# One group of four heads' keys and queries: transposed on TensorE, or loaded as token rows and transposed by DMA

## The chip, the cores and the metric

The kernel runs on one core of a Trainium2 chip. The metric is the device time of one execution in microseconds (us), as the median of several runs. A profile is one further execution with every instruction recorded.

## The reference

Causal attention with an additive bias that falls with a running sum, followed by a layer norm and a two-layer network with a residual. Batch 8, 8 heads, 576 tokens, 64 dimensions per head, model width 512, hidden width 2048.

```python
def _attn_ref(q, k, v, s):
    scores = scale * np.matmul(q, k.transpose(0, 1, 3, 2))
    cum = np.cumsum(np.maximum(s, 0.0), axis=-1)
    bias = -(cum[:, :, :, None] - cum[:, :, None, :])
    scores = np.where(causal, -1000000000.0, scores + np.minimum(bias, 0.0))
    scores = scores - np.max(scores, axis=-1, keepdims=True)
    attn = np.exp(scores)
    attn = attn / (np.sum(attn, axis=-1, keepdims=True) + 1e-09)
    return np.matmul(attn, v)
def _moe_ref(x, g_ln, w_ch1, w_ch2):
    xn = (x - mu) / np.sqrt(var + 1e-06) * g_ln
    return x + np.maximum(xn @ w_ch1, 0.0) @ w_ch2
```

For the scores TensorE needs q and k with the 64 dimensions of a head (and four rows that carry the bias) on the partitions and the tokens along the free axis. In memory they lie the other way round: tokens outside, dimensions inside. So every head's q and k have to be transposed somewhere.

## The kernel before

The order of the work is written out by hand: one loop over `n` (line 745), 64 steps, one for each head of each batch (`b, h = n // 8, n % 8`). A step emits `pre(n)` (line 675), which holds loads and casts for later steps; then the scores of its head (`scores`, line 304, three PSUM banks called `sa`, `sb`, `sc`, each turned into weights `er` by an exponential on ACT, line 323, and masked by POOL, line 331); then pieces of the network of the batch before (`run_units`: `mlp1` writes `ph`, line 497; `mlp2` writes `py`, line 515, and DVE finishes the rows in `yo`, line 524, which SP stores, line 542); and from step 10 on the product with the values of the head two steps back (`pv`, line 378, matmuls at line 389). Every engine and every DMA queue executes its instructions in the order in which they are written.

Heads go in groups of four, `gam = n // 4` (16 groups). A group's q and k stand transposed in one of two buffers, `kq[gam % 2]`, 68 partitions high: 64 dimensions and four rows of bias. There are two ways to fill it.

- **By TensorE** (groups 0 to 5, that is batches 0 to 2). Two heads at a time, "pairs" `g`, two pairs to a group. `ld_cast_pair` (line 130) has POOL issue two DMAs, k and q, which load f32 and write bf16, six consecutive tokens to a partition (96 partitions). `tr_pair` (line 243) issues 12 transposes on TensorE (line 255) into two PSUM tiles `trqk`; `evac_pair` (line 262) copies them to `kq` in four copies, for the later pairs two on DVE (line 100) and two on ACT (line 98). `PAIR_LOADS` (line 671) says in which step a pair is loaded, `PAIRS` (line 672) in which it is transposed. The bias rows come by four small DMAs on SP, `aug` (line 207; lines 210 and 212), which wait until the group before in the same buffer has been read.
- **By DMA** (groups 6 to 15). `ld_rows` (line 159) loads 128 tokens of four heads, k and q, with two DMAs on SP (line 164) into a staging tile `rowtmp`, from the pool of six that the values' loads (`vtmp`, line 139) use too. `cast_rows` (line 172) has POOL cast it to bf16 (line 176) and copy the bias columns next to it (line 177) into one of four `rows` buffers. `tr_rows` (line 182) issues one DMA transpose on SP (line 186), 128 tokens by 8 head-halves, into `kq`. A group needs five of each; steps `4 gam - 6` to `4 gam - 2` hold them (lines 706 to 721). The transposed tiles lie tile by tile, so a range of queries that runs past token 512 is read with two matmuls in place of one (`q_cols`, line 289).

`NPE = 3` (line 49) is the number of batches that go by TensorE. The four `rows` buffers get their unused columns zeroed once, by POOL, in step 16 (line 701). `cT`, the bias columns, is filled in steps 9 and 12.

Of the kernel before, what the change touches and what calls it, by code (L numbers as in the profile page):

```python
# [19 lines left out]
def kernel(  # L20
# [25 lines left out]
    EW = 1664  # L46
    G = 4
    NG = BH // G
    NPE = 3
    NM = 10  # L50
    NR = 4
    QT = 6
# [77 lines left out]
    def ld_cast_pair(g):  # L130
        ld_cast("k", g)
        ld_cast("q", g)

    def ld_v(b, t):
        if b >= B:
            return
        pn = P if t < NF else TL
        tmp = stage.tile([P, H, D], F32, name="vtmp", tag="st")
        nc.sync.dma_start(
            out=tmp[:pn], in_=v[b, :, t * P : t * P + pn, :].rearrange("h s d -> s h d")  # L140
        )
        loaded["v", b, t] = tmp


    def ld_cast_v(b, t):
        pn = P if t < NF else TL
        nc.gpsimd.dma_start(
            out=v_bf[b % 2][:pn, t, :, 0:D],
            in_=v[b, :, t * P : t * P + pn, :].rearrange("h s d -> s h d"),
        )  # L150

    def cast_v(b, t, eng):
        if b >= B:
            return
        pn = P if t < NF else TL
        copy_on(eng, v_bf[b % 2][:pn, t, :, 0:D], loaded.pop(("v", b, t))[:pn])


    def ld_rows(gam, t):
        pn = P if t < NF else TL  # L160
        b, h0 = gam // 2, (gam % 2) * G
        tmp = stage.tile([P, 2, G, D], F32, name="rowtmp", tag="st")
        for u, src in enumerate((k, q)):
            nc.sync.dma_start(
                out=tmp[0:pn, u],
                in_=src[b, h0 : h0 + G, t * P : t * P + pn, :].rearrange("h s d -> s h d"),
            )
        loaded["rows", gam, t] = tmp
# [3 lines left out]
    def cast_rows(gam, t):  # L172
        pn = P if t < NF else TL
        r = rows[turn[0] % NR]
        turn[0] += 1
        nc.gpsimd.tensor_copy(out=r[0:pn, :, :, 0:D], in_=loaded.pop(("rows", gam, t))[0:pn])  # L176
        nc.gpsimd.tensor_copy(
            out=r[0:pn, :, :, D:KA], in_=cT[0:pn, t, :, gam * G : (gam + 1) * G, :]
        )
        ready["rows", gam, t] = r  # L180

    def tr_rows(gam, t):
        pn = P if t < NF else TL
        r = ready.pop(("rows", gam, t))
        o = t * 2 * G * P
        nc.sync.dma_start_transpose(
            out=kq[gam % 2]
            .rearrange("p u h s -> p (u h s)")[:, o : o + 2 * G * pn]
            .rearrange("p (h s) -> p h s", s=pn),
            in_=r[0:pn].rearrange("p u h c -> p (u h c)"),  # L190
        )
# [4 lines left out]
    def ld_w1(c):  # L196
        sl = slice(c * 512, (c + 1) * 512)
        nc.gpsimd.dma_start(out=w1_bf[:, :, sl], in_=w1_r[:, :, sl])

    def ld_w2(i):  # L200
        nc.gpsimd.dma_start(
            out=w2_bf[:, 4 * i : 4 * i + 4, :], in_=w2_r[:, 4 * i : 4 * i + 4, :]
        )
# [3 lines left out]
    def aug(gam, eng, h0=0):  # L207
        r = slice(gam * G + h0, gam * G + G)
        i = gam % 2
        eng.dma_start(out=kq[i][D : D + 1, 1, h0:G, 0:S], in_=c_hi[r, :])  # L210
        for j in range(3):
            eng.dma_start(out=kq[i][D + 1 + j : D + 2 + j, 0, h0:G, 0:S], in_=c3[r, j, :])
# [62 lines left out]
    def qk_pair(g, k_engs, q_engs):  # L275
        tr_pair(g)
        evac_pair("k", g, k_engs)
        evac_pair("q", g, q_engs)


    def k_cols(b, h, kb):
        i, hh = (b * 2 + h // G) % 2, h % G
        if b < NPE:
            return kq[i][0:KA, 0, hh, kb * P : (kb + 1) * P]
        n = P if kb < NF else TL
        o = kb * 2 * G * P + hh * n
        return kq[i].rearrange("p u h s -> p (u h s)")[0:KA, o : o + P]

    def q_cols(b, h, q0, q1):
        i, hh = (b * 2 + h // G) % 2, h % G  # L290
        if b < NPE:
            return [(q0, q1, kq[i][0:KA, 1, hh, q0:q1])]
        flat = kq[i].rearrange("p u h s -> p (u h s)")
        full = flat[0:KA, 0 : NF * 2 * G * P].rearrange("p (t h s) -> p t h s", t=NF, s=P)
        o = NF * 2 * G * P + (G + hh) * TL
        got = []
        if q0 < NF * P:
            qf = min(q1, NF * P)
            got.append((q0, qf, full[:, q0 // P : qf // P, G + hh, :]))
        if q1 > NF * P:  # L300
            got.append((NF * P, q1, flat[0:KA, o : o + TL]))
        return got

    def scores(b, h):
        e = er[:, h % 4, :]
        pe_mask = b * H + h < NM

        def bank(name, blocks, o):
            a = ps_s.tile([P, 512], F32, name=name, tag="s")
            for c, kb, q0, q1, diag in blocks:  # L310
                for a0, a1, cols in q_cols(b, h, q0, q1):
                    nc.tensor.matmul(  # L312
                        a[:, c + a0 - q0 : c + a1 - q0],
                        lhsT=k_cols(b, h, kb),
                        rhs=cols,
                        start=True,
                        stop=not (pe_mask and diag),
                    )
                if pe_mask and diag:
                    nc.tensor.matmul(  # L320
                        a[:, c : c + P], lhsT=ident, rhs=maskT, start=False, stop=True
                    )
            nc.scalar.activation(out=e[:, o : o + 512], in_=a, func=ACT.Exp, scale=scale)  # L323

        bank("sa", ((0, 0, 0, 512, True),), 0)
        bank("sb", ((0, 0, 512, 576, False), (64, 1, 128, 576, True)), OB)
        bank("sc", ((0, 2, 256, 576, True), (320, 3, 384, 576, True)), OC)
        if pe_mask:
            return
        for o in (0, OB + 64, OC, OC + 320):  # L330
            nc.gpsimd.affine_select(  # L331
                out=e[:, o : o + P],
                in_=e[:, o : o + P],
                compare_op=ALU.is_ge,
                fill=0.0,
                base=0,
                pattern=[[1, P]],
                channel_multiplier=-1,
            )
# [328 lines left out]

    PAIR_LOADS = {11: 8, 12: 9, 13: 10, 16: 11}
    PAIRS = {9: 5, 11: 6, 13: 7, 14: 8, 15: 9, 16: 10, 21: 11}


    def pre(n):
        if n == 0:
            nc.vector.memset(mhalf, -0.5)
            ld_cast_pair(4)
        elif n == 1:
            ld_w1(1)  # L680
        elif n == 3:
            ld_cast_pair(5)
            for t in range(NT):
                ld_cast_v(1, t)
        elif n == 4:
            ld_w1(2)
            ld_w1(3)
        elif n == 7:
            ld_cast_pair(6)
            ld_w2(0)  # L690
            ld_cast_pair(7)
            ld_w2(1)
        elif n == 10:
            ld_w2(2)
            ld_w2(3)
        elif n == 12:
            nc.vector.memset(cT[:, :, 0, :, 0], -1.0)
            nc.vector.memset(cT[:, :, 1, :, 1:4], 1.0)
        elif n == 16:
            for r in rows:  # L700
                nc.gpsimd.memset(r[:, :, :, KA:P], 0.0)
        if n in PAIR_LOADS:
            ld_cast_pair(PAIR_LOADS[n])
        if n % 4 == 0 and 2 <= n // 4 + 1 < 2 * NPE:
            aug(n // 4 + 1, nc.sync)
        for gam in range(2 * NPE, NG):
            m = n - 4 * gam
            if m == -6:
                ld_rows(gam, 0), ld_rows(gam, 1)
            elif m == -5:  # L710
                cast_rows(gam, 0), cast_rows(gam, 1)
                ld_rows(gam, 2), ld_rows(gam, 3)
            elif m == -4:
                tr_rows(gam, 0), tr_rows(gam, 1)
                cast_rows(gam, 2), cast_rows(gam, 3)
                ld_rows(gam, 4)
            elif m == -3:
                tr_rows(gam, 2), tr_rows(gam, 3)
                cast_rows(gam, 4)
            elif m == -2:  # L720
                tr_rows(gam, 4)
        for nb in range(2, B):
            m = n - H * nb + (5 if nb == 2 else 7)
            if 0 <= m < NT:
                ld_v(nb, m)
            if 1 <= m <= NT:
                cast_v(nb, m - 1, "pool")
# [17 lines left out]
    for n in range(BH):  # L745
        b, h = n // H, n % H
# [62 lines left out]
        nu = (2 if n < 16 else -(-len(queue) // (end - n + 1))) - 2  # L809
        if n in PAIRS:  # L810
            qk_pair(PAIRS[n], ("dve", "dve"), ("act", "act"))
        scores(b, h)
# [63 lines left out]
```

## Time and profile before

| What | Value |
|---|---|
| median of 5 runs | 368.65 us (367.83 to 372.14) |
| the profiled execution's own time | 367.83 us |
| its span, first to last instruction | 366.1 us |
| PE busy | 357.7 us, 98% of the span |
| DVE, ACT, POOL busy | 205.8, 194.2, 161.5 us |
| granted TensorE clock | 1.0 |
| DMA packets | 147981, of which 134185 under 512 bytes |

PE is TensorE's matmuls, PEld its weight loads, DVE VectorE, ACT ScalarE, POOL GpSimd; SPq is the queue of DMAs that SyncE issues. Times in a timeline are microseconds from the start of the span. In a timeline's line stand the start, the duration of the merged pieces, the engine, the line of the kernel, the operation, the tile written and the tiles read, the shape and the count; a bracket at the end is the idle time of the engine before it, and what ended it. A matmul's recorded duration includes its way through the pipeline, so the pace of TensorE is read from the distance between starts.

### The profile page before, as it was taken

Reading aid. Unit: us, or ns where it says so; the run is one execution under the profiler, and the core shown is the slowest. Engines: PE = TensorE matmul, PEld = TensorE weight load, DVE = VectorE, ACT = ScalarE, POOL = GpSimd, SP = SyncE. Lnnn points to the kernel's source line nnn. Section 1 sums busy time; section 2 is a strip of 40 time slices with the busy share of each in tenths; the row PEclk is TensorE's granted clock in tenths of the full one; section 3 lists DMA queues with packets and bytes.
Section 4 is the critical chain, followed back from the end, with each engine's and each line's share of the span. In section 5 each row is a group of like instructions: output and inputs, shape, how many; then the busy total and the mean of one; then the engine's idle time right before and its main releaser. Section 6 shows DMA issues by size and latency. Waiting matters only on the chain.

```text
span 366.1 us, 8372 instructions
## 1 busy us (share of the span) xinstructions
PE 357.7 (98%) x3079; PEld 197.7 (54%) x3079; DVE 205.8 (56%) x539; ACT 194.2 (53%) x371; POOL 161.5 (44%) x441
## 2 busy tenths in 40 slices
PE   8999999999999999999999999999999999999995
PEld 3676555565555555555555555555555554444444
DVE  7697789786448453944394547643665483112211
ACT  5895998568733674357534753476347422501410
POOL 8954475757643646454754563555552101000000
PEclk9999999999999999999999999999999999999999
DMA  8999994679965999599869998898730011011013
GB/s 149 161 193 182 202 214 74 136 194 171 178 134 134 215 189 186 116 242 178 182 160 221 181 183 141 201 206 185 146 100 2 0 60 57 3 57 57 3 29 86
DMA packets 147981, 50.42 MB, mean 138 GB/s; under 512 B 134185, under 2 KB 143268, under 8 KB 147940
## 3 DMA queue, kind: packets, MB, share of 16 engines
q1 hardware_dynamic: 129364, 40.74, 52.3%
q0 software_dynamic: 18176, 8.62, 19.4%
q10 hardware_dynamic: 400, 0.52, 0.5%
q8 instruction: 24, 0.39, 0.4%
q14 instruction: 17, 0.14, 0.1%
HBM read 37.11 MB, written 9.44 MB: 127 GB/s over the span
## 4 chain that ended last, share of the span: by engine, by line
PE 80%; DVE 10%; DMA 3%; ACT 2%; issue 1%; SPq 1%; POOL 1%; ACTq 0%; POOLq 0%
PE py L515 31%; PE ph L497 27%; PE pot L389 6%; PE sc L312 3%; PE sb L312 3%; PE sa L312 3%; PE idle L568 2%; DVE xn L451 2%; PE trx L484 2%; DVE stats L423 2%; DVE kq L100 2%; DMA kq<-rows 1%; DVE xb L399 1%; PE trqk L255 1%; ACT er L323 1%
## 5 line engine op out<-in xcount | busy, mean ns | idle before, releaser
L515 PE MATMUL py<-w_bf,hT 128*128 128x512 bf16 (+1 forms) x592 | 136.5, 373 | 0.4 <-DVE yo L524 0.4
L497 PE MATMUL ph<-xT,w_bf 128*128 128x512 bf16 x496 | 117.8, 379 | 0.1
L507 ACT ACTIVATE hT<-ph 128x512 bf16<-128x512 f32 x102 | 61.0, 598 | 62.8 <-PE ph L497 62.8
L515 PEld LDWEIGHTS <-hT 128*128 128x128 bf16 x592 | 53.5, 98 | 49.0 <-issue 0.9
L497 PEld LDWEIGHTS <-w_bf 128*128 128x128 bf16 x560 | 50.3, 97 | 51.7 <-issue 3.3
L323 ACT ACTIVATE er<-sa 128x512 bf16<-128x512 f32 x64 | 38.2, 597 | 69.7 <-PE sa L312 42.2
L331 POOL TENSOR_SCALAR_AFFINE_SELECT er<-er 128x128 bf16<-128x128 bf16 x216 | 58.8, 296 | 26.6 <-ACT er L323 26.4
L505 DVE TENSOR_SCALAR hT<-ph 128x512 bf16<-128x512 f32 x38 | 26.3, 692 | 54.6 <-PE ph L497 49.1
L176 POOL CAST rows<-rowtmp 128x512 bf16<-128x512 f32 (+1 forms) x50 | 30.4, 608 | 48.4 <-DMA rowtmp<-in_q_dram 47.0
L312 PEld LDWEIGHTS <-kq 68*128 68x128 bf16 x440 | 32.8, 97 | 26.3 <-issue 1.4
L389 PEld LDWEIGHTS <-er 128*128 128x128 bf16 x960 | 37.4, 98 | 14.2 <-issue 0.7
L389 PE MATMUL pot<-v_bf,er 128*128 128x65 bf16 x960 | 39.6, 193 | 0.1
L397 DVE RECIPROCAL rinv<-pot 128x5 f32<-128x5 f32 x64 | 12.3, 192 | 47.8 <-PE pot L389 47.5
L323 ACT ACTIVATE er<-sc 128x512 bf16<-128x512 f32 x64 | 39.0, 610 | 0.0
L524 DVE SCALAR_TENSOR_TENSOR yo<-py,rstd,xb 128x512 f32<-128x512 f32 x32 | 24.0, 749 | 25.5 <-PE py L515 20.8
L323 ACT ACTIVATE er<-sb 128x512 bf16<-128x512 f32 x64 | 38.3, 598 | 0.1
L399 DVE TENSOR_TENSOR xb<-pot,rinv 128x256 f32<-128x256 f32 x64 | 27.2, 425 | 2.2
L439 POOL TENSOR_TENSOR rstd<-rstd,mhalf 128x4 f32<-128x4 f32 (+1 forms) x8 | 8.8, 1096 | 42.5 <-DVE rstd L438 42.5
L102 POOL CAST v_bf<-vtmp 128x512 bf16<-128x512 f32 (+1 forms) x30 | 18.4, 612 | 16.3 <-DMA vtmp<-in_v_dram 16.3
L423 DVE BATCH_NORM_STATS2 stats<-xb 128x6 f32<-128x128 f32 (+2 forms) x100 | 25.3, 312 | 0.4
L312 PE MATMUL sc<-kq 68*128 68x256 bf16 (+1 forms) x208 | 25.2, 232 | 0.3
L312 PE MATMUL sb<-kq 68*128 68x64 bf16 (+1 forms) x168 | 24.4, 246 | 0.4 <-ACT hT L797 0.2
(101 smaller groups left out, 332.0 us busy)
## 6 DMA issues: line engine op xcount, KB each, us to landing
out_dram<-yo SPq DMA_DIRECT2D x32, 256.0 KB
vtmp<-in_v_dram SPq DMA_DIRECT2D x24, 256.0 KB
rowtmp<-in_k_dram SPq DMA_DIRECT2D x40, 128.0 KB
rowtmp<-in_q_dram SPq DMA_DIRECT2D x40, 128.0 KB
w_bf<-in_moe_w_ch_dram POOLq DMA_DIRECT2D x8, 512.0 KB, 10.6
kp<-in_k_dram POOLq DMA_DIRECT2D x11, 144.0 KB, 6.2
qp<-in_q_dram POOLq DMA_DIRECT2D x11, 144.0 KB, 6.7
v_bf<-in_v_dram POOLq DMA_DIRECT2D x8, 128.0 KB, 8.0
```

Source lines behind the costliest of these rows:

```text
L176: nc.gpsimd.tensor_copy(out=r[0:pn, :, :, 0:D], in_=loaded.pop(("rows", gam, t))[0:pn])
L312: nc.tensor.matmul(a[:, c + a0 - q0 : c + a1 - q0], lhsT=k_cols(b, h, kb), rhs=cols, start=True, stop=not (pe_mask and diag),)
L323: nc.scalar.activation(out=e[:, o : o + 512], in_=a, func=ACT.Exp, scale=scale)
L331: nc.gpsimd.affine_select(out=e[:, o : o + P], in_=e[:, o : o + P], compare_op=ALU.is_ge, fill=0.0, base=0, pattern=[[1, P]], channel_mult ...
L389: nc.tensor.matmul(pot[:, t, :], lhsT=e[:, o : o + P], rhs=vv[:, kb, h, :], start=(kb == 0), stop=(kb == last),)
L399: nc.vector.tensor_tensor(out=xb[b][:, :, hs], in0=pot[:, 0:NF, 0:D], in1=rinv[:, 0:NF].unsqueeze(2).to_broadcast([P, NF, D]), op=ALU.mult,)
L423: nc.vector.bn_stats(out=st[b][:, t, part, :], in_=x[:, lo:hi])
L497: nc.tensor.matmul(ph, lhsT=w1_bf[:, kd, fb * P : (fb + 1) * P], rhs=xT[:, kd, :], start=(kd == 0), stop=(kd == KD - 1),)
L505: nc.vector.tensor_scalar_max(out=hT[:, fb, :], in0=ph, scalar1=0.0)
L507: nc.scalar.activation(out=hT[:, fb, :], in_=ph, func=ACT.Relu)
L515: nc.tensor.matmul(py[0], lhsT=hT[:, fb, t * P : (t + 1) * P], rhs=w2_bf[:, fb, c0:c1], start=(fb == 0), stop=(fb == FB - 1),)
L524: nc.vector.scalar_tensor_tensor(out=yo, in0=py[0], scalar=rs, in1=x[:, c0:c1], op0=ALU.mult, op1=ALU.add)
```

## The change

Group 5 (heads 4 to 7 of batch 2, steps 20 to 23) goes the second way in place of the first. `NPE` now counts groups of four heads, not batches, and is 5. Pairs 10 and 11 are neither loaded nor transposed on TensorE, `aug(5)` is gone, and the loop over groups that go by DMA starts at 5, so that group 5's loads, casts and DMA transposes stand in steps 14 to 18. The zeroing of the `rows` buffers moves from step 16 to step 14.

```diff
-    NPE = 3
+    NPE = 5
@@ k_cols
-        if b < NPE:
+        if b * 2 + h // G < NPE:
@@ q_cols
-        if b < NPE:
+        if b * 2 + h // G < NPE:
@@
-    PAIR_LOADS = {11: 8, 12: 9, 13: 10, 16: 11}
-    PAIRS = {9: 5, 11: 6, 13: 7, 14: 8, 15: 9, 16: 10, 21: 11}
+    PAIR_LOADS = {11: 8, 12: 9}
+    PAIRS = {9: 5, 11: 6, 13: 7, 14: 8, 15: 9}
@@ pre
-        elif n == 16:
+        elif n == 14:
             for r in rows:
                 nc.gpsimd.memset(r[:, :, :, KA:P], 0.0)
@@
-        if n % 4 == 0 and 2 <= n // 4 + 1 < 2 * NPE:
+        if n % 4 == 0 and 2 <= n // 4 + 1 < NPE:
             aug(n // 4 + 1, nc.sync)
-        for gam in range(2 * NPE, NG):
+        for gam in range(NPE, NG):
             m = n - 4 * gam
             if m == -6:
                 ld_rows(gam, 0), ld_rows(gam, 1)
```

## The prediction

> **What bounds the kernel now.** I read the page first, for the engine that is busy; then the busy times by stretch of 10 us; then TensorE's timeline at the two places where the change takes transposes out; then the chain and the queue of SP for what could be late instead.
>
> The page's first and second parts: busy time of TensorE, and in 40 slices of 9.15 us its busy share, the granted clock and the DMA engines' share.
>
> ```profile
> PE 357.7 (98%) x3079; PEld 197.7 (54%) x3079; DVE 205.8 (56%) x539; ACT 194.2 (53%) x371; POOL 161.5 (44%) x441
> PE   8999999999999999999999999999999999999995
> PEclk9999999999999999999999999999999999999999
> DMA  8999994679965999599869998898730011011013
> ```
>
> TensorE is the bound and its clock is full throughout. A busy share of 98% alone does not say that its pace is not set by others, so the stretches around the change (columns: PE, PEld, DVE, ACT, POOL busy, clock, DMA share, GB/s):
>
> ```profile
> 50.00:60.00 10.00, 9.25 (x117) 5.96 (x116) 9.52 (x20) 8.41 (x16) 7.66 (x22) 1.00 1.04 174
> 60.00:70.00 10.00, 9.82 (x91) 5.46 (x89) 7.96 (x21) 7.79 (x14) 6.71 (x19) 1.00 0.33 59
> 70.00:80.00 10.00, 10.00 (x101) 5.90 (x100) 9.05 (x26) 5.23 (x11) 3.93 (x10) 1.00 0.74 186
> 80.00:90.00 10.00, 9.92 (x94) 5.65 (x92) 6.09 (x15) 8.48 (x16) 7.90 (x22) 1.00 0.99 184
> ```
>
> From 66 us on TensorE has work without a gap (10.00 of 10 in most stretches to 240), so work taken from it there shortens the run one for one, unless another queue then becomes late. Between 60 and 70 the DMA engines are a third busy: that is the room for the new transfers. Between 50 and 60 they are full.
>
> TensorE's timeline at step 16 (pair 10) and step 21 (pair 11), and, for the form that replaces them, the scores of step 24, the first group that goes by DMA:
>
> ```profile
> 62.74 0.42 PE L255 MATMUL trqk<-ident,kp 96*128 96x96 bf16 x6
> 63.00 0.42 PE L255 MATMUL trqk<-ident,qp 96*128 96x96 bf16 x6
> 63.26 0.38 PE L312 MATMUL sa<-kq 68*128 68x512 bf16 x1
> ...
> 65.12 0.22 PE L347 MATMUL sd<-kq 68*128 68x64 bf16 x2 [0.18 <-ACT kq L98]
> ...
> 85.14 0.42 PE L255 MATMUL trqk<-ident,kp 96*128 96x96 bf16 x6
> 85.40 0.42 PE L255 MATMUL trqk<-ident,qp 96*128 96x96 bf16 x6
> 85.65 0.38 PE L312 MATMUL sa<-kq 68*128 68x512 bf16 x1
> ...
> 99.65 0.38 PE L312 MATMUL sa<-kq 68*128 68x512 bf16 x1
> 99.87 0.38 PE L312 MATMUL sb<-kq 68*128 68x64 bf16 x3
> 100.09 0.39 PE L312 MATMUL sc<-kq 68*128 68x256 bf16 x4
> 100.31 1.03 PE L515 MATMUL py<-w_bf,hT 128*128 128x512 bf16 x4
> ```
>
> The distance of starts is what counts: 12 transposes take 62.74 to 63.26, 0.52 us, and 85.14 to 85.65, 0.51. The duration column (0.42 for six) would say 0.84.
>
> **The change, part by part.**
>
> *TensorE, removed.* 24 transposes: 0.52 + 0.51 = 1.03 us. Also the 0.18 us at 65.12: `sd` waits there for ACT's copy of pair 10 because it needs that pair's PSUM tile. With pair 10 gone it takes a tile of pair 9, whose copies ended by 62.8 (DVE 61.22 for 1.62 us) and 61.7 (ACT 60.10 for 1.61). Together 1.21 us, none of it beside other TensorE work.
>
> *TensorE, added.* Three extra matmuls per head, 12 in all (448 columns become 384 and 64; 320 become 256 and 64; 192 become 128 and 64), each with a weight load. The columns stay the same. Lower bound 0: in step 24 the split banks are 0.22 us apart (99.87, 100.09, 100.31), and in step 22, by the old form, 90.68, 90.90, 91.11, the same. Upper bound: a weight load (98 ns by the group of line 312) and 30 ns of matmul (the two of `sd`, 82.04 to 82.10) each, uncovered: 12 x 0.13 = 1.5 us. I take 0, since step 24 is the same code and sits in the same order.
>
> *DVE and ACT, removed.* Four copies each of 0.80 us, 3.2 us on each engine. Not the bound; their worth is the wait above. DVE's first `yo` came at 66.69, right after pair 10's copies; it can come nearer to its `py`.
>
> *POOL.* Out go four DMA issues (0.64 us each, 2.6 us), in come five casts and five bias copies (0.60 + 0.20 us, 4.0 us): +1.4 us over steps 13 to 17. By step: 13, -1.3; 14, +1.8 (the zeroing moved there); 15, +1.6; 16, -1.5 (two casts in, zeroing and two issues out); 17, +0.8. Behind these in POOL's order stand the masks of the same step, and for them `pv` waits two steps later. In step 14 POOL was idle 1.49 us before its mask at 57.98, so the zeroing ends about 57.7, the value cast 58.3, and the mask is 0.3 us late; in step 15 it was idle 2.10 us before 62.40, so 1.6 fit. `pv` of step 14 runs at 66.04, masks done about 60: 6 us of cover. Cost 0.
>
> *SP's queue.* Out go `aug(5)`'s four DMAs (60.75 to 63.2). In come ten row loads (about 0.5 us each to issue) and five transposes. SP's rows for the next group show the pattern and its price:
>
> ```profile
> 81.66 3.48 SPq L186 DMA_TRANSPOSE kq<-rows  x2
> 85.20 0.69 SPq L164 DMA_DIRECT2D rowtmp<-in_k_dram  x1
> 87.82 2.76 SPq L186 DMA_TRANSPOSE kq<-rows  x2
> 91.42 1.26 SPq L186 DMA_TRANSPOSE kq<-rows  x1
> ```
>
> Worked forward for group 5: tiles 0 and 1 are loaded in the crowded stretch, issued from 50 us behind two value loads; there `vtmp` loads took 5.4 to 8.4 us to land (semaphore updates in the trace), so they land by 58.4, before POOL's turn at 59.7. The first transposes must wait until step 15's scores have read `kq[1]` (60.6, where `aug(5)` was released) and for POOL's casts (61.3 or a little later), and take 3.5 us to issue: 65. Tile 4's loads go out 65 to 66.2 and land in 2.4 (the same loads at 85.20): 68.6. Step 16's output store follows at 66.4, transposes 2 and 3 until 69.6, the value load until 70.1, the next store 70.5, and the last transpose goes at about 70.6, its cast done at 69.4. Transposes land 2.65 to 5.98 us after issue in this trace; at 2.95, as the fifth of group 6 (91.42 to 94.37), that is 73.6. Step 20's scores read them at 80.52 - 0.70 = 79.8. Slack 6 us. What is queued behind the waiting transposes: two output stores and group 6's loads, about 1 us later than before (71.18), for casts that POOL reaches only at 80.88. Three `yo` buffers stand between a late store and DVE, so TensorE sees nothing of it. Cost 0.
>
> *DMA traffic.* The bytes from memory are the same; transposes and small packets come on top, mostly in the third-busy stretch. That steals nothing from a transfer on the path as far as the rows show. The transfers of pair 9 (issued 49.48 and 50.10, landed 55.7 and 56.8) share that stretch with the first row loads and are due at 59.08: 2.3 us of cover. Bounds: 0, and 2 us if they were slowed like the slowest load there (8.40 us in place of 6.7: 58.5, still in time). I take 0.
>
> A rule against the change: the Trainium skill, "VectorE: DVE Perf Modes", section "The three transpose paths", gives 390 ns for a 128x128 transpose on TensorE and 1309 ns by DMA, and advises TensorE wherever PSUM will do as a target. Taken as costs in series, an estimate, 24 transposes would free 9.4 us and 36 blocks by DMA would need 47 us, past the due time by 28. The trace disagrees on both: 43 ns apiece on TensorE (0.52 us for 12), and eight blocks landed within 2.65 to 5.98 us by DMA.
>
> *Sum.* 0.52 + 0.18 + 0.51 = 1.21 us off. The profiled execution took 367.83 us (span 366.1, 1.7 around it) and would take 366.6; it was the fastest of the five, 0.82 under the median. The median goes from 368.65 to 367.4.
>
> **The rivals.**
>
> *A, cancelled: the split matmuls are not free, or the gain is given back further on.* At the upper bound above, 1.5 us, they eat the gain: 368.9; at half, 368.2. Against it: the equal spacing at step 24. For giving back: the rows of group 12 were already late once:
>
> ```profile
> 208.36 0.61 POOL v_bf L102
> 209.27 4.64 DMA kq<-rows
> 214.57 0.86 PE py L515 x4
> ```
>
> with 0.6 us of idle before step 48's scores. But that chain starts at a `yo` at 195.21, so it moves with TensorE. About 368.6.
>
> *B, slower: group 5 is late at step 20.* A new wait of TensorE on the transposes. By the worst rows throughout: tile 4's load takes 8.4 us (66.2 to 74.6), cast 0.8, transpose 5.98: 81.4, 1.6 us late, hence 368.65 - 1.21 + 1.6 = 369.0. It decides the sign once the last transpose lands after 81.0, and to lose 1% it would have to land after 84.7. Against it: the DMA engines are a third busy there.
>
> *C, more gain.* Other small gaps close as well: the 0.6 us at step 48 if the phases shift favourably. 368.65 - 1.8 = 366.8.
>
> *The change does nothing.* Excluded: the new program's instruction lists have 24 transposes, four copies on DVE and four on ACT fewer.
>
> **How the numbers follow.** The sum as forecast 0.60; A 0.17; B 0.13; C 0.10. Predicted is the first, 367.4, by itself 366.8 to 368.0. The five runs lie within 1.1 us but for one, so a median is good to some 0.5 us. The range takes in C less that (366.2) and B plus a little (369.2). About 1%, 3.7 us, is what a measurement of this kernel can tell from no change: none of the cases reaches that; what I leave for it is B in a form that lasts over several groups (0.07), and a gain by something I do not see (0.02). Within 1%: 0.91.
>
> **What would show each step.** Right: steps 16 and 21 begin with `sa` directly, no idle before `sd` of step 16, `sa` of step 22 about 1.2 us earlier (before, 90.46); the split banks of steps 20 to 23 0.22 us apart; the last transpose of group 5 landed by 76; no idle of line 312 on `kq<-rows` at step 20. Wrong: such an idle, TensorE waiting for POOL's masks in steps 16 to 19, pair 9's transposes waiting for their loads at 59, or gaps at later groups that before had none (steps 24, 28, 36, 44), which would mean that the row pipeline and not TensorE sets the pace.

## The result, and the profile after

The changed kernel takes 367.51 us (median of 49 runs, 366.58 to 372.73); the kernel before, 368.48 us (91 runs). The ratio is 0.9976, with a 95% interval of 0.9966 to 0.9986: 0.9 us faster, between 0.5 and 1.25. Predicted were 367.4 us, a range of 366.2 to 369.2 and, from 367.4 to 368.65, a ratio of 0.9966.

The profiled execution of the changed kernel took 369.71 us (span 368.0), more than the median and more than the profiled execution of before. The reason lies ahead of the change, in steps 1 to 4. Busy times of the changed kernel in stretches of 2 us (columns as before):

```profile
14.00:16.00 2.00, 1.89 (x19) 1.26 (x20) 0.16 (x1) 1.41 (x3) 1.68 (x3) 0.98 1.63 140
16.00:18.00 2.00, 2.00 (x22) 1.69 (x19) 0.35 (x1) 1.77 (x5) 1.23 (x2) 0.50 1.22 213
18.00:20.00 2.00, 2.00 (x29) 1.59 (x27) 1.96 (x3) 1.32 (x3) 1.84 (x3) 0.66 1.10 223
```

```profile
14.11 0.39 PE L312 MATMUL sa<-kq 68*128 68x512 bf16 x1 [1.58 <-DMA kq<-c]
```

The second fence is TensorE's timeline at step 1: it waited 1.58 us for bias rows from a DMA, and from 15.94 us on ran for 3.4 us at half its clock. By step 6 this execution is 2.95 us behind that of before, and still is at step 15 (2.94). No instruction of the two kernels differs there. So the change is read from the distances between steps, not from the spans.

TensorE's timeline of the changed kernel at the two places (columns as before):

```profile
62.84 0.38 PE L312 MATMUL sa<-kq 68*128 68x512 bf16 x1
...
65.68 0.38 PE L312 MATMUL sa<-kq 68*128 68x512 bf16 x1
65.90 0.38 PE L312 MATMUL sb<-kq 68*128 68x64 bf16 x2
66.31 0.38 PE L312 MATMUL sc<-kq 68*128 68x320 bf16 x2
66.53 1.03 PE L515 MATMUL py<-w_bf,hT 128*128 128x512 bf16 x4
67.39 0.22 PE L347 MATMUL sd<-kq 68*128 68x64 bf16 x2
...
70.50 0.38 PE L312 MATMUL sa<-kq 68*128 68x512 bf16 x1
...
82.80 0.38 PE L312 MATMUL sa<-kq 68*128 68x512 bf16 x1
83.02 0.38 PE L312 MATMUL sb<-kq 68*128 68x64 bf16 x3
83.23 0.39 PE L312 MATMUL sc<-kq 68*128 68x256 bf16 x4
...
87.43 0.38 PE L312 MATMUL sa<-kq 68*128 68x512 bf16 x1
...
90.27 1.89 PE L497 MATMUL ph<-xT,w_bf 128*128 128x512 bf16 x8
92.00 0.38 PE L312 MATMUL sa<-kq 68*128 68x512 bf16 x1
```

No transposes, no idle before `sd`, split banks 0.21 and 0.22 apart. Of the kernel before, the prediction shows the first scores of steps 16 and 21 (63.26 and 85.65); the other lines needed are these:

```profile
59.91 0.38 PE L312 MATMUL sa<-kq 68*128 68x512 bf16 x1
...
68.22 0.38 PE L312 MATMUL sa<-kq 68*128 68x512 bf16 x1
...
80.52 0.38 PE L312 MATMUL sa<-kq 68*128 68x512 bf16 x1
...
88.49 2.13 PE L497 MATMUL ph<-xT,w_bf 128*128 128x512 bf16 x8
90.46 0.38 PE L312 MATMUL sa<-kq 68*128 68x512 bf16 x1
```

From one step's first scores to the next's:

| Distance | before | after | gained |
|---|---|---|---|
| step 15 to 16 (holds pair 10's transposes) | 3.35 | 2.84 | 0.51 |
| step 16 to 17 (holds the `sd` wait) | 4.96 | 4.82 | 0.14 |
| step 20 to 21 (holds pair 11's transposes) | 5.13 | 4.63 | 0.50 |
| step 21 to 22 | 4.81 | 4.57 | 0.24 |

1.39 us, by unrounded starts 1.40. The second row hides two parts. From `py` to `sd` it was 1.21 us (63.91 to 65.12) and is now 0.86 (66.53 to 67.39): 0.35 gained. Of this 0.20 goes back ahead of `sc`, which now starts 0.41 us after `sb` in place of 0.21; in the trace it is released by ACT's exponential of step 15's `sc`, which ends at 66.26. With step 16 half a microsecond earlier, TensorE catches up with ACT there.

The fourth row was not in the prediction. The second `ph` group of step 21 shows it in the kernel before: eight matmuls spread over 2.13 us in place of 1.89. The fifth of them starts at 89.60, released by ACT's ReLU.

From step 22 to 39 the two kernels keep step. Then rows come late in each, though at different groups. The waits of TensorE for rows between 100 us and 300 us (total, times, longest), the changed kernel first:

```profile
PEld L312 <- DMA kq<-rows: 0.7, 1, 0.7
PE sb L312 <- DMA kq<-rows: 0.2, 1, 0.2
```

and before:

```profile
PEld L312 <- DMA kq<-rows: 0.6, 1, 0.6
```

The changed kernel loses 0.66 us of pace at step 40, the kernel before 0.32 at step 48. That is 1.40 - 0.66 + 0.32 = 1.06 us between the two profiles, within the interval of what was timed.

### The profile page after: what moved, and what is told of

It reads as the page before. It is cut to its first block, busy times and chain, and to the rows that moved or that the text cites. A ratio compares the mean times of both kernels' runs of the same rounds, so it can differ in the third digit from the quotient of the medians.

```text
span 368.0 us, 8365 instructions
## 1 busy us (share of the span) xinstructions
PE 358.3 (97%) x3067; PEld 198.4 (54%) x3067; DVE 202.8 (55%) x535; ACT 191.6 (52%) x367; POOL 165.1 (45%) x447
## 4 chain that ended last, share of the span: by engine, by line
PE 81%; DVE 8%; DMA 5%; ACT 2%; SPq 1%; issue 1%; POOL 1%; POOLq 0%; ACTq 0%
PE py L515 31%; PE ph L497 29%; PE pot L389 7%; PE sc L312 3%; PE sb L312 3%; PE sa L312 3%; DVE xn L451 2%; DMA rowtmp<-in_q_dram 2%; PE trx L484 2%; DMA kq<-c 1%; ACT er L323 1%; DVE stats L423 1%; PE trqk L255 1%; ACT kq L98 1%; DMA kq<-rows 1%
## 5 line engine op out<-in xcount | busy, mean ns | idle before, releaser
L331 POOL TENSOR_SCALAR_AFFINE_SELECT er<-er 128x128 bf16<-128x128 bf16 x216 | 59.7, 300 | 23.8 <-ACT er L323 23.7
L176 POOL CAST rows<-rowtmp 128x512 bf16<-128x512 f32 (+1 forms) x55 | 33.7, 613 | 48.8 <-DMA rowtmp<-in_q_dram 45.6
L312 PEld LDWEIGHTS <-kq 68*128 68x128 bf16 x452 | 33.7, 98 | 28.2 <-issue 2.2
L312 PE MATMUL sa<-kq 68*128 68x512 bf16 x64 | 24.6, 385 | 1.7 <-DMA kq<-c 1.6
```

The source lines that it names most:

```text
L312: nc.tensor.matmul(a[:, c + a0 - q0 : c + a1 - q0], lhsT=k_cols(b, h, kb), rhs=cols, start=True, stop=not (pe_mask and diag),)
L331: nc.gpsimd.affine_select(out=e[:, o : o + P], in_=e[:, o : o + P], compare_op=ALU.is_ge, fill=0.0, base=0, pattern=[[1, P]], channel_mult ...
```

## The experiments

Three theories. Theory 1: the gain is TensorE's own time, and group 5's row path costs nothing. Theory 2, the rival: the row path of group 5 eats part of the gain. Theory 3: rows that come late at steps 40, 48 or 56, in groups that the change does not touch, hide part of it. Ratios are to the kernel before on the same chip, with 95% intervals. "Pace lost" is by how much the distance between two steps exceeds that of the same steps in a run without the wait.

**Removal alone.** Heads 4 to 7 of batch 2 are computed from whatever the buffer held.

```diff
-    PAIR_LOADS = {11: 8, 12: 9, 13: 10, 16: 11}
-    PAIRS = {9: 5, 11: 6, 13: 7, 14: 8, 15: 9, 16: 10, 21: 11}
+    PAIR_LOADS = {11: 8, 12: 9}
+    PAIRS = {9: 5, 11: 6, 13: 7, 14: 8, 15: 9}
```

> The kernel before without pairs 10 and 11: neither loaded, transposed nor copied, and nothing in their place, so heads 4 to 7 of batch 2 are computed from what the buffer held. This is the removal by itself. Theory 1 (TensorE's own time is all of the gain, the row path costs nothing): step 15 to step 22 shorter by 1.4 us (1.03 transposes, 0.18 at the sd of step 16, 0.24 at the second group of ph in step 21), and the time the same as that of the changed kernel, ratio to before about 0.997. Theory 2 (part of the gain is eaten by the row path of group 5): clearly faster than the changed kernel, 0.996 or less, and the changed kernel's 1.4 us at step 22 is lost later.

Measured: 367.08 us, 0.9979 (0.9958 to 1.0001). Steps 15 to 22 are 1.42 us shorter, the changed kernel's 1.40. Late rows cost 0.67 us at step 48 here. With nothing put in the place of the pairs the kernel is no faster than with the row path, within 0.2%. That is 0.8 us, more than the 0.5 us that theory 2 would explain; what speaks against theory 2 is the pace, and that rows come late here too, without any rows of group 5.

**The split reads.**

```diff
-            return [(q0, q1, kq[i][0:KA, 1, hh, q0:q1])]
+            cuts = [q0, NF * P, q1] if b * H + h >= NM and q0 < NF * P < q1 else [q0, q1]
+            return [(a, z, kq[i][0:KA, 1, hh, a:z]) for a, z in zip(cuts, cuts[1:])]
```

> The kernel before, with the query ranges of heads 10 to 23 cut at token 512 as the row form cuts them: 42 more matmuls and weight loads, all else as it was. Theory 1 (split is free): ratio 1.000 and banks 0.22 us apart. Theory 2 (each costs an uncovered weight load and 30 ns, 0.13 us): 42 x 0.13 = 5.5 us slower, ratio 1.015; the 12 of the change would then have cost 1.5 us.

Measured: 1.0014 (1.0001 to 1.0027), against the 1.015 of an uncovered weight load. A batch 2 head with its split banks:

```profile
73.30 0.38 PE L313 MATMUL sa<-kq 68*128 68x512 bf16 x1
73.52 0.38 PE L313 MATMUL sb<-kq 68*128 68x64 bf16 x3
73.74 0.39 PE L313 MATMUL sc<-kq 68*128 68x256 bf16 x4
73.96 1.03 PE L516 MATMUL py<-w_bf,hT 128*128 128x512 bf16 x4
```

0.22 us a bank, as uncut; and from step 9 to 24 the pace differs from that of before by 0.07 us for 42 added matmuls. By the pace the change's twelve cost 0.02 us; by the timed ratio, at its middle, 0.0014 x 368.2 x 12 / 42 = 0.15 us. Rival A's 1.5 is out.

**The row path added, nothing taken out.** First try:

```diff
+    spare = const.tile([P, 2, S], BF16, name="spare")
+    PAIR_LOADS = {11: 8, 12: 9, 13: 10, 16: 11}
+    PAIRS = {9: 5, 11: 6, 13: 7, 14: 8, 15: 9, 16: 10, 21: 11}
...
+        to = spare[0:D] if g > 9 else kq[(g // 2) % 2][0:D, "kq".index(kind), hh : hh + 2, 0:S]
```

> The changed kernel, with the loads, transposes and copies of pairs 10 and 11 done as well, in their old steps, into a spare tile that nobody reads: the row path added, nothing taken out but the four bias DMAs. Theory 1: the same as before, 1.000 (within 0.1%). Theory 2: slower than before by what the row path costs, 0.4 us or more (1.001 or over).

Measured: 372.55 us, 1.0118 (1.0085 to 1.0151). That would speak for theory 2, but the wait names my own edit:

```profile
67.60 0.23 PE L347 MATMUL sd<-kq 68*128 68x64 bf16 x2 [1.79 <-DVE spare L101]
```

k (by DVE) and q (by ACT) went to one spare tile, so ACT waited for DVE, and TensorE for the PSUM tile. The two idle stretches (1.79 and 0.79) make 2.6 of the 4.4 us. Besides these the profiled execution (371.74 us) has 0.86 us by step 4, ahead of the edit, and 0.93 from late rows at steps 40 and 56. Second try, a tile for each:

```diff
-    spare = const.tile([P, 2, S], BF16, name="spare")
+    spare = const.tile([P, 2, 2, S], BF16, name="spare")
-        to = spare[0:D] if g > 9
+        to = spare[0:D, "kq".index(kind)] if g > 9
```

> As the run with rows added, but keys and queries of pairs 10 and 11 are copied to separate spare tiles, so that ACT's copies no longer wait for DVE's (in the first form they wrote one tile, and TensorE idled 1.79 us at step 16 and 0.79 at step 21 for that alone). The row path of group 5 added, nothing taken out but the four bias DMAs. Theory 1 (the row path costs nothing): steps 15 to 22 as before, ratio 1.000 within 0.15%. Theory 2 (it costs what is missing between 1.4 and 0.9): 1.001 to 1.002, and idle of TensorE in steps 14 to 24 that the kernel before has not.

Measured: 368.60 us, 1.0008 (0.9993 to 1.0022). Between steps 15 and 24 it is 0.02 us behind the pace of before. The ten loads, ten POOL operations and five transposes of group 5 cost TensorE nothing where they stand. The timed ratio alone does not decide, since its interval reaches from theory 1's 1.000 over theory 2's 1.001 to 1.002; the pace speaks against theory 2.

**Values later.**

```diff
-            m = n - H * nb + (5 if nb == 2 else 7)
+            m = n - H * nb + (5 if nb == 2 else 6)
```

> The changed kernel, with the value loads and casts of batches 3 to 7 one step later, so that on SP the last value load of a batch stands behind the last transpose of the even group and not ahead of it. In the profiles one even group was late at its scores in each (step 48 before, 0.3 us of pace lost; step 40 after, 0.7 us). Theory 1 (these late rows are what separates the 1.4 us at step 22 from the 0.9 to 1.0 measured): no late rows at steps 32, 40, 48, 56 and a ratio of 0.996. Rival (they come from loads that wait elsewhere, or are too rare to count): 0.9976 as the changed kernel, and idle at such steps still.

Measured: 368.14 us, 1.0002 (0.9983 to 1.0022): slower than the changed kernel if anything. It lost 0.51 us at step 40 and 0.65 at step 48. The order was not what I expected. The queue of SP ahead of step 48:

```profile
206.10 3.00 SPq L186 DMA_TRANSPOSE kq<-rows  x2
209.15 0.57 SPq L139 DMA_DIRECT2D vtmp<-in_v_dram  x1
209.81 1.28 SPq L186 DMA_TRANSPOSE kq<-rows  x1
```

A value load still stands ahead of the fifth transpose, now one of 128 tokens in place of 64.

**Rows earlier.** For groups 6 to 15:

```diff
+            if gam > NPE:
+                if m == -7:
+                    ld_rows(gam, 0), ld_rows(gam, 1)
+                elif m == -6:
+                    ld_rows(gam, 2), ld_rows(gam, 3)
+                elif m == -5:
+                    cast_rows(gam, 0), cast_rows(gam, 1)
+                    ld_rows(gam, 4)
+                elif m == -4:
+                    tr_rows(gam, 0), tr_rows(gam, 1)
+                    cast_rows(gam, 2), cast_rows(gam, 3)
+                elif m == -3:
+                    tr_rows(gam, 2), tr_rows(gam, 3)
+                    cast_rows(gam, 4)
+                    tr_rows(gam, 4)
+                continue
```

> The changed kernel, for groups 6 to 15: the row loads one step earlier, and the fifth transpose right behind the third and fourth, ahead of the value load. In every profile so far one to three of the steps 40, 48, 56 waited for rows, 0.3 to 1.3 us of pace in total. Theory 3 (that is lateness of SP's queue): no such waits, ratio 0.9955 to 0.997. Rival (SP and the DMA engines are full, so earlier loads push something else back): waits elsewhere, 0.9976 or more.

Measured: 366.73 us, 0.9962 (0.9948 to 0.9977): faster than before, and below the changed kernel's 0.9976, though the two intervals overlap. The same edit on the kernel before, and once more on the changed one, on one chip:

> The kernel before with the rows of groups 6 to 15 loaded a step earlier and the fifth transpose right behind the fourth, and nothing of the change. Theory 3 (every run of every kernel here loses 0.3 to 1.3 us to late rows, whether the change is in or not, and this lateness hides part of the difference): ratio 0.999 and no idle on rows; the same edit on the changed kernel is then 1.4 us below it, 0.4%. Rival (the lateness is the changed kernel's own): ratio 1.000, and less than 1.4 us between the two.

> The changed kernel with earlier rows once more, beside the kernel before with earlier rows on the same chip, to read the difference of the two. Theory 3: 0.9962 as the first time, 1.4 us below the other. Rival: 0.9970 or more, the first time having been luck.

Measured: 1.0003 (0.9995 to 1.0012) without the change and 0.9959 (0.9947 to 0.9971) with it, medians 368.25 and 366.62. The change is worth 1.6 us between these two. TensorE's waits for other engines in the changed kernel with earlier rows, second run (50 to 300 us):

```profile
PEld L484 <- DVE xn L451: 0.6, 2, 0.4
PE py L515 <- DVE yo L524: 0.4, 2, 0.2
PE sd L347 <- ACT kq L98: 0.4, 1, 0.4
PE trqk L255 <- ACT er L358: 0.2, 1, 0.2
```

None on `kq<-rows`; its span is 364.7 us, and steps 15 to 22 are 1.40 us shorter than before. From step 15 to the last, its pace is 0.66 us ahead of the changed kernel's, and all of that arises at steps 39 to 41, where the changed kernel waited for rows. So theory 3 holds for the changed kernel. For the kernel before it does not: I expected 0.999, and earlier rows gain it nothing. The profiled execution of that kernel ran at about a sixth of the usual speed throughout, and nothing is read from it.

**Slack of group 5.**

```diff
-            m = n - 4 * gam
+            m = n - 4 * gam - (2 if gam == NPE else 0)
```

> The changed kernel with all of group 5's loads, casts and transposes two steps later (steps 16 to 20). In the changed kernel's profile the fifth transpose landed 5.6 us before step 20's scores began. Theory 1 (that is slack): two steps are 8.6 us, so TensorE waits about 3 us at step 20, ratio about 1.006. Rival B of the prediction (there is little slack, because a later load also lands later): over 6 us, ratio 1.014 or more.

Measured: 379.45 us, 1.030 (1.028 to 1.032). The rival's number: 11 us, where it said over 6 and theory 1 about 3. TensorE at step 20:

```profile
85.54 0.59 PE L312 MATMUL sa<-kq 68*128 68x512 bf16 x1 [4.21 <-DMA kq<-rows]
90.77 0.58 PE L312 MATMUL sb<-kq 68*128 68x64 bf16 x3 [4.64 <-DMA kq<-rows]
...
91.59 1.89 PE L497 MATMUL ph<-xT,w_bf 128*128 128x512 bf16 x4
```

8.85 us of waits in place of 3, and on top the clock: the four matmuls of `ph` at 91.59 take 1.89 us where eight do at full clock. The rival's reason, a load that lands later, was not it: the fifth tile's two loads landed 2.6 and 2.4 us after issue, as in the changed kernel. The queue shows why the waits are longer than two steps less the slack of 5.6:

```profile
74.89 0.87 SPq L164 DMA_DIRECT2D rowtmp<-in_k_dram  x1
75.82 0.60 SPq L164 DMA_DIRECT2D rowtmp<-in_q_dram  x1
76.47 0.61 SPq L164 DMA_DIRECT2D rowtmp<-in_k_dram  x1
...
80.07 3.27 SPq L186 DMA_TRANSPOSE kq<-rows  x2
83.39 0.58 SPq L164 DMA_DIRECT2D rowtmp<-in_k_dram  x1
```

The lines at 74.89 and 75.82 are group 5's fifth tile; those from 76.47 up to the transposes are group 6's first two. The fifth tile's transpose is issued only at 87.32, behind the transposes of 80.07, four more loads of group 6 from 83.39, a value load and an output store. Group 5's last loads now stand among group 6's, and each row step passes SP and POOL in turn behind the other group's. So slack measured at one place in a queue is not delay that the queue can take.

**Group 4 by DMA as well.** `NPE` 4, no pair loads after pair 7, the bias columns and the zeroing in step 10.

```diff
-    NPE = 5
-    PAIR_LOADS = {11: 8, 12: 9}
-    PAIRS = {9: 5, 11: 6, 13: 7, 14: 8, 15: 9}
+    NPE = 4
+    PAIR_LOADS = {}
+    PAIRS = {9: 5, 11: 6, 13: 7}
```

> The changed kernel with group 4 (heads 0 to 3 of batch 2) by DMA too; the bias columns and the zeroing of the row buffers move to step 10. Theory 1 (each group saves TensorE's transposes and the waits on their tiles): in steps 14 and 15 another 1.03 us of transposes go and the waits 0.39, 0.21 and 0.14 there, 1.8 us, ratio 0.993. Rival (the DMA engines are full until step 14, so the rows are late): idle on the rows at step 16, ratio 0.9976 or more.

Measured: 373.22 us, 1.0143 (1.0121 to 1.0165). The rival, and more than it said. POOL and TensorE:

```profile
53.69 0.61 POOL L176 CAST rows<-rowtmp 128x512 bf16<-128x512 f32 x1 [3.48 <-DMA rowtmp<-in_q_dram]
```

```profile
62.97 1.11 PE L389 MATMUL pot<-v_bf,er 128*128 128x65 bf16 x15 [1.36 <-POOL er L331]
64.26 0.38 PE L312 MATMUL sa<-kq 68*128 68x512 bf16 x1 [0.18 <-DMA kq<-rows]
66.05 0.61 PE L312 MATMUL sb<-kq 68*128 68x64 bf16 x3 [1.41 <-DMA kq<-rows]
...
66.89 1.90 PE L515 MATMUL py<-w_bf,hT 128*128 128x512 bf16 x4
```

One row load issued at 42.9 landed 12.5 us later. POOL waits for it in order, the masks stand behind the cast, `pv` behind the masks. Against before, steps 13 and 14 gained 1.6 us; step 15 lost 1.8, mostly the wait for the masks, and step 16 lost 4.1: 1.41 waiting for rows, the rest mostly at half clock (eight matmuls' time, 1.90 us, for four of `py` at 66.89).

**ACT's copies alone.** Two copies put back on ACT at step 21, reading the buffer:

```diff
+        if n == 21:
+            for w in range(2):
+                nc.scalar.copy(out=spare[0:D, w], in_=kq[0][0:D, 1, 2 * w : 2 * w + 2, 0:S])
```

> The changed kernel with two copies of the size of pair 11's (64x576, 0.8 us each) put back on ACT at step 21, from the buffer to a spare tile, and nothing else of the pair. Theory 1 (of the 0.75 us that step 21 lost, 0.51 is transposes and 0.24 is TensorE waiting for a PSUM tile that ACT's ReLU, behind these copies, frees late): step 21 is 0.24 us longer than in the changed kernel, 4.80 from its first scores to step 22's in place of 4.57. Rival (the 0.24 belongs to the transposes): 4.57.

Measured: 376.98 us, one run. By step 21 that buffer belongs to group 6, and ACT waited for its transposes:

```profile
92.30 2.20 ACT L813 COPY spare<-kq 64x1152 bf16<-64x1152 bf16 x2 [6.72 <-DMA kq<-rows]
```

It says nothing on the 0.24. With a weight tile as source:

```diff
+                nc.scalar.copy(out=spare[0:D, w, 0:832], in_=w1_bf[0:D, w, 0:832])
```

> As the run with copies put back on ACT, but they read a weight tile and not the buffer, which by then belongs to the next group (there ACT waited 6.7 us for group 6's transposes, and TensorE 7.8 for ACT). Two ACT copies of about 0.8 us at step 21, nothing else of pair 11. Theory 1 (0.24 us of step 21's 0.75 is TensorE waiting for a PSUM tile behind ACT's copies): step 21 is 4.80 us long, from its first exponential's place to step 22's 0.24 more than in the changed kernel. Rival (it belongs to the transposes): as in the changed kernel, 4.57.

Measured, in one run (368.35 us): step 21 takes 5.20 us (85.37 to 90.57), 0.63 more than in the changed kernel. Theory 1 said 4.80, the rival 4.57.

```profile
85.37 0.38 PE L313 MATMUL sa<-kq 68*128 68x512 bf16 x1
...
88.22 1.03 PE L498 MATMUL ph<-xT,w_bf 128*128 128x512 bf16 x4
89.71 1.02 PE L498 MATMUL ph<-xT,w_bf 128*128 128x512 bf16 x4 [0.46 <-ACT hT L508]
90.57 0.38 PE L313 MATMUL sa<-kq 68*128 68x512 bf16 x1
```

The mechanism of theory 1 is there, named in the bracket: ACT's ReLU comes late behind the copies, and TensorE lacks a tile for `ph`. The size is above 0.24. What fits it is that here the copies begin 0.69 us after the step's first scores, in the kernel before 0.20 after, and take 0.08 us longer each; this was not tested by itself.

## Why the prediction was right, point by point

- **TensorE's transposes, 1.03 us.** Measured 0.51 + 0.50. Reading the pace from starts and not from durations was what made this right.
- **The wait of `sd`, 0.18.** Gone; the step gained 0.14. That the two are close is luck: 0.18 is the idle time in the bracket, by starts the wait had cost 0.35, and 0.20 of it came back as a wait for ACT ahead of `sc`, which the prediction did not foresee.
- **DVE and ACT, "their worth is the wait above".** Wrong by 0.24 us. ACT's copies of pair 11 also delayed its ReLUs at step 21 (from 85.85 to 90.15 ACT has no gap over 0.03 us), and TensorE waited for the PSUM tile that the first of them frees. The line was in the trace (2.13 for eight matmuls), and I read only the wait beside the transposes. The removal is worth 1.40 us locally, not 1.21.
- **The split matmuls, 0.** 0.02 us by the pace of 42 added ones.
- **POOL, SP and DMA traffic, 0.** Right at the place: 0.02 us up to step 24 with the row path added. The fifth transpose landed at 77.2, 5.6 us ahead of step 20's scores, where 6 was forecast.
- **The sum.** 1.21 forecast, 0.9 (0.5 to 1.25) measured. Two errors of opposite sign, so the closeness of the total is partly luck: 0.2 us of gain missed, and about 0.5 us given back, by the runs to late rows. The second is rival A's "given back further on", which I had at 0.17 and dismissed because the chain at step 48 begins at a `yo` and so moves with TensorE. In the profiles it does not simply move along: the wait at step 48 is gone, as rival C had it, and a longer one stands at step 40, where the kernel before had none. A gap at a later group that before had none was the prediction's own sign that rows, and not TensorE, set the pace there; it named steps 24, 28, 36 and 44, and these stayed clean. With late rows removed, the change is worth 1.6 us between two medians (0.0044 of ratio, 0.003 to 0.006), without, 0.9.
- **Rival B, slower.** Did not happen; its price was too low. Each microsecond of wait was taken as a microsecond; in the two runs where rows were late by more than a microsecond (group 5 two steps late, group 4 by DMA), TensorE's clock halved on top.

What stays open: why the kernel before loses less to late rows. In the profiles it lost 0.32 us, the changed kernel 0.66, the removal alone 0.67; one execution each is too little, and earlier rows left the kernel before where it was. That the faster TensorE leaves the queue less time fits these three, but not the rest: runs whose TensorE is no faster lost 0.47 (split reads) and 0.54 us (rows added, second try) to late rows at step 56. How much of the 0.5 us is the change's own doing, and how much differs from one execution to the next, is not shown.

## What to carry to other kernels

When an engine at 98% loses an instruction, count what the instruction's helpers held up as well: the copies behind 24 transposes were worth 0.4 us of waits beside 1.03 of transposes. Test a small gain once more with the nearest other wait taken away; here moving unrelated loads one step earlier raised the change from 0.24% to 0.4% and gave the fastest version (366.6 to 366.7 us). And do not extend a move into a stage whose transfers are full: the same step one group earlier turned the gain into 1.4% of loss.

## What was not expected of the hardware

TensorE's granted clock fell to half after short waits. In the changed kernel's profile one wait of 1.58 us at step 1 was followed by 3.4 us at half clock, with a loss of 2.95 us in all; in the run with group 4 by DMA, waits of 1.36, 0.18 and 1.41 us within 5 us went with 6.8 us at half clock, which began during the third; one of 1.79 us, in the first run with rows added, was followed by none. Each stretch at half clock is a multiple of 3.41 us (3.41, 6.83, and 10.24 in the run with group 5 two steps late).

```profile
64.00:66.00 2.00, 0.45 (x4) 0.10 (x1) 1.79 (x8) 0.60 (x1) 0.51 (x1) 0.81 0.93 202
66.00:68.00 2.00, 1.96 (x10) 1.06 (x11) 0.18 (x1) 1.08 (x2) 1.95 (x8) 0.50 1.00 225
68.00:70.00 2.00, 2.00 (x8) 0.75 (x7) 0.75 (x1) 0.27 (x1) 0.92 (x4) 0.50 1.08 241
70.00:72.00 2.00, 1.78 (x18) 1.25 (x18) 0.50 (x2) 0.00 (x0) 1.60 (x6) 0.50 1.14 214
72.00:74.00 2.00, 2.00 (x14) 1.02 (x13) 0.41 (x2) 0.15 (x1) 1.34 (x5) 0.98 1.24 180
```

These are the stretches of the run with group 4 by DMA; the clock is the third column from the end.

The traces also show what sets the longer wait apart. The half-clock stretches begin a whole number of 3.413 us after TensorE first got its full clock: 5.70 + 3 x 3.413 = 15.94 in the changed kernel's profile, 7.21 + 17 x 3.413 = 65.23 in that with group 4 by DMA. So count TensorE's idle time in windows of 3.413 us from that first moment, over all the profiles but the one at a sixth of the speed. Of the windows at full clock none with up to 1.36 us of idle was followed by half clock, and each with 1.95 or more was. Between these both occur: 1.58, 1.74 and 1.83 were followed by half clock, 1.73 to 1.88 in the last windows of four other runs were not. The wait of 1.58 us lies whole in one window; that of 1.79 us lies across two, which have 0.80 and 1.05.

The Trainium skill, "TensorE: Matmul & The Clock Gate", section "Why this matters for your kernels", asks for no gaps above some 3 us to keep the clock. The same page, section "What's actually happening", explains the gate by activity windows of about 3.4 us that run on their own. The windows fit what was measured here; the 3 us do not, since 1.58 us within one window was enough.
